# Even shares for the convolutions from slot 36 on, and a step-by-step pace for decoding layer 2's weights

## The chip, the cores and the metric

The kernel runs on one core of one Trainium2 chip. Five engines of that core take part, each with its own queue, in order: TensorE (PE in the profile, with its weight loads as PEld), VectorE (DVE), ScalarE (ACT), GpSimd (POOL) and SyncE (SP), which issues most of the DMAs. [...] The metric is device microseconds of one execution. The kernel before took 1217.21 us, the median of 2 runs (1216.93 to 1217.49).

## The reference

Input x is 2 x 4096 x 192 in float32. Three stages follow one another:

- a causal depthwise convolution of 7 taps: the taps are a softmax of `weight` (8 heads x 7), and each head serves 24 of the 192 channels;
- layer 1, on the 8192 rows: `h = x @ w_in` (192 x 2048), `g = h * clip(h + 3, 0, 6) / 6`, `y = g @ w_out` (2048 x 192);
- layer 2, of the same sizes with its own weights: `h = y @ w_in`, `g = h` where h is positive and `exp(h) - 1` elsewhere, `out = g @ w_out`.

The weights arrive as float64, so a float32 pair of words must be decoded into a float32 on the chip before they can be used.

## The kernel before

**Blocks and slots.** The 8192 rows are cut into 16 blocks of 512 (256 of each batch). In each layer the 2048 hidden columns are cut into 16 tiles f of 128. One slot is one (layer, block, f): `mm1` (L437) makes h of that tile in a PSUM bank, `gate` (L461) turns it into g, `split_g` (L473) splits g into a high part gh and a rest gl, and `mm2` (L482), four slots later (LAG), adds the tile's share of the output. The list `slots` (L497) has 512 entries: slots 0 to 31 hold blocks 0 and 1 of layer 1, interleaved; 32 to 95 hold blocks 2 to 5 of layer 1, 16 slots each; from 96 on layers 2 and 1 alternate by block: layer 2 block 0 in 96 to 111, layer 1 block 6 in 112 to 127, layer 2 block 1 in 128 to 143, and so on.

**Exactness.** Each product is made from high and low parts, so a slot has five matmuls of `mm1` and five of `mm2`. From slot 36 on (BOTH + LAG, L706) they are issued as two streams of half height, lower and upper rows of the array, whose matmuls run side by side; the lower stream is 8 matmuls ahead (BEHIND). There an `mm1` has 5 matmuls in one half and 4 in the other: 19 half matmuls a slot, 9.5 pairs. Three banks hold h (`ps_h`, L100).

**What runs beside the matmuls.** For each slot ACT makes u and gh, DVE g and gl. The rest are jobs, generators whose steps are dealt out slot by slot:

- `weights` (L597): decodes 30 items, 16 of layer 1 and then 14 of layer 2, sorted by the slot in which they are first needed. Items 16, 17 and 18, the first of layer 2, are w_in of tiles 0 to 3, the last 64 rows of w_in of tiles 0 to 7, and w_in of tiles 4 to 7. An item takes four steps: `decode` (L117) scales one word on ACT and shifts the other on DVE (tensor_scalar), then come the rest of the split of the item before, and two DVE combinations. `split_w` (L157) copies the high part on ACT and subtracts on DVE.
- `feed(b)` (L324): 12 DMAs on SP that bring block b of x. `squares(b)` (L270): two DVE transposes. `conv(b)` (L315): 20 steps; `taps_vector` (L275) has one product on ACT and six multiply-adds (acc) on DVE for each of two parts (512 and 256 elements), taken in turn; then come the operands of `mm1`: opA (ACT), opB (DVE), and opC and opD, which need ACT copies (L308 to L312), two DVE subtractions (L313, L314, step 19) and two more ACT copies of their results (L316, L317, step 20).
- the end of a block: `upper_sum` (L362, the rest of the sums y, s and yr) and, for layer 2, `split_y` (L418).

**The planner.** `run_jobs` (L524) is called once a slot, behind g of this slot and gl of the one before. A job has a first slot a, a deadline e and a number of steps n. It is forced in slot e - 2 (e - 1 where e is at most 32). Before slot 112 (OWN) it otherwise gets a step only while the estimated debt of DVE and ACT is low (L535); from slot 112 on it gets its even share of the slots from a to e (L536). Among the jobs that want a step, the one with the earliest deadline goes first. The deadline of `weights` is `when(ready)` (L562), where `ready` is the item last decoded; for layer 2 it rises evenly from slot 40 to 112 (W2). For blocks 2 to 6 the deadline of the convolution is the first slot of its block, but slot 104 for block 6.

The work ahead of slot 36 is not issued in the order of the text: the framework packs it, engine by engine, when the program is built, and there later steps can fill an engine's gaps. From slot 36 on the order is that of the text (`tc.manual_schedule`, L706).

```
        def wanted(jb):
            e, a, _, n, done = jb
            if s >= e() - (1 if e() <= BOTH else 2):
                return True
            if s < OWN:
                return s >= a and debt[0] < 0 and debt[1] < 500
            return done * (e() - a) < n * (s - a + 1)
```

Of the kernel before, what the change touches and what calls it, by code (L numbers as in the profile page):

```python
# [17 lines left out]
P = 128  # L18
LAG = 4
BEHIND = 8  # L20
RA = 6
# [2 lines left out]
FIRST0 = 1  # L24
FIRST = 5
TENSOR_TAPS = 2
OWN = 112
W2 = (40, 112)
R_CUTS = ((4, 4, 8), (8,))
PACE = 1900  # L30
NB = 512
# [26 lines left out]
def conv_moe_moe2(ctx: ExitStack, tc: tile.TileContext, x, weight, w_in1, w_out1, w_in2, w_out2, out):  # L58
# [18 lines left out]
    B, S, D = x.shape  # L77
# [3 lines left out]
    NF = FF // P  # L81
    PAD = K - 1
    G = D // H
    R = D - P
# [29 lines left out]
    def word(raw, i):  # L114
        return raw.rearrange("p (n two) -> p n two", two=2)[:, :, i]

    def decode(raw, n, meanwhile):  # L117

        xw = tmp.tile([P, NB], F32, name="xw", tag="xw")
        act.mul(xw[:, :n], word(raw, 1).bitcast(F32), 2.0 ** -112)
        c = tmp.tile([P, NB], I32, name="cw", tag="cw")
        vec.tensor_scalar(out=c[:, :n], in0=word(raw, 0).bitcast(U32), scalar1=2.0 ** -29, scalar2=7.0,
                          op0=ALU.mult, op1=ALU.min)
        yield
        yield from meanwhile
        xi = xw.bitcast(I32)
        vec.scalar_tensor_tensor(out=c[:, :n], in0=xi[:, :n], scalar=3, in1=c[:, :n],  # L130
                                 op0=ALU.logical_shift_left, op1=ALU.bitwise_or)
        yield
        vec.scalar_tensor_tensor(out=xi[:, :n], in0=xi[:, :n], scalar=SIGN, in1=c[:, :n],
                                 op0=ALU.bitwise_and, op1=ALU.bitwise_or)
        yield
        return xw
# [20 lines left out]
    def split_w(item, f):  # L157

        kind, l, a, e = item
        if kind == "out":
            v = f[:, :(e - a) * D].rearrange("p (f e) -> p f e", f=e - a)
            w = wo[l][:, a:e]
            act.copy(w[:, :, 0:D], v)
            yield
            for c0, c1, to in ((0, P, 2 * P), (P, D, D)):
                vec.tensor_tensor(out=w[:, :, to:to + c1 - c0], in0=v[:, :, c0:c1],
                                  in1=w[:, :, c0:c1].bitcast(F32), op=ALU.subtract)
            yield  # L170
            return
        w = {k: v[:, a * P:e * P] for k, v in wi[l].items()}
        if kind == "in":
            f = f[:, :(e - a) * P]
            act.copy(w["h"], f)
            yield
            vec.tensor_tensor(out=w["l"], in0=f, in1=w["h"].bitcast(F32), op=ALU.subtract)
        else:
            f = f[:, :(e - a) // 2 * P].rearrange("p (f c) -> p f c", c=P)
            r = w["r"].rearrange("p (f two c) -> p two f c", two=2, c=P)  # L180
            for k, h in enumerate((LO, UP)):
                act.copy(r[h, k], f[h])
            yield
            for k, h, o in ((0, LO, UP), (1, UP, LO)):
                vec.tensor_tensor(out=r[o, k], in0=f[h], in1=r[h, k].bitcast(F32), op=ALU.subtract)
        yield
# [83 lines left out]
    def squares(b):  # L270
        for part, t in enumerate(x_sb.pop(b)):
            vec.transpose(out=halves(b, part), in_=t)
            yield
# [31 lines left out]
    def conv_r(b):  # L305
        a = yield from taps_vector(b, 1)
        lh, hl = opnd[0, b][2:]
        T0, T1 = slice(0, HB), slice(HB, NB)  # L308
        act.copy(hl[LO, T0], a[LO])
        act.copy(lh[UP, T1], a[UP])  # L310
        yield
        act.copy(lh[UP, T0], a[LO])  # L312
        act.copy(hl[LO, T1], a[UP])  # L313
        yield  # L314
        vec.tensor_tensor(out=lh[LO, T0], in0=a[LO], in1=hl[LO, T0].bitcast(F32), op=ALU.subtract)  # L315
        vec.tensor_tensor(out=hl[UP, T1], in0=a[UP], in1=lh[UP, T1].bitcast(F32), op=ALU.subtract)  # L316
        yield  # L317
        act.copy(hl[UP, T0], lh[LO, T0].bitcast(F32))
        act.copy(lh[LO, T1], hl[UP, T1].bitcast(F32))
        yield  # L320

    def conv(b):
        opnd[0, b] = ring()
        yield from alternate(conv_main(b, taps_tensor if b < TENSOR_TAPS else taps_vector), conv_r(b))  # L324
# [12 lines left out]
    def feed(b):  # L337
        load_squares(b)
        yield
# [166 lines left out]
    at = {sl: i for i, sl in enumerate(slots)}  # L506
# [11 lines left out]
    def job(gen, n, a, e):  # L518

        jobs.append([e if callable(e) else lambda: e, a, gen, n, 0])  # L520
# [3 lines left out]
    def run_jobs(s, before):  # L524


        for i, (eng, w) in enumerate(zip((vec, act), before)):
            debt[i] = min(max(debt[i] - PACE, -PACE), -PACE // 2) + eng.work - w

        def wanted(jb):  # L530
            e, a, _, n, done = jb
            if s >= e() - (1 if e() <= BOTH else 2):
                return True
            if s < OWN:
                return s >= a and debt[0] < 0 and debt[1] < 500  # L535
            return done * (e() - a) < n * (s - a + 1)  # L536

        while True:
            todo = [j for j in jobs if wanted(j)]
            if not todo:  # L540
                break
            jb = min(todo, key=lambda j: j[0]())
            w = vec.work, act.work
            if next(jb[2], jobs) is jobs:
                jobs.remove(jb)
            jb[4] += 1
            debt[0] += vec.work - w[0]
            debt[1] += act.work - w[1]

    def whole(*gens):  # L550
        for g in gens:
            yield from g
# [5 lines left out]
    def due(item):  # L558
        kind, l, a, e = item
        return at[l, 0, a] + (LAG if kind == "out" else 0)  # L560

    def when(i):  # L562

        if i >= len(items):
            return 0
        if i < N1:
            return due(items[i]) - LEAD
        return min(due(items[i]) - LEAD, W2[0] + (W2[1] - W2[0]) * (i - N1) // (len(items) - N1))

    def cuts(*steps):  # L570
        out, a = [], 0
        for n in steps:
            while a < NF:
                out.append((a, a + n))
                a += n
                if n != steps[-1]:
                    break
        return out

    items = [("in", l, a, e) for l in range(2) for a, e in cuts(*((2, 2, 4) if l == 0 else (4,)))]  # L580
    items += [("r", l, a, e) for l in range(2) for a, e in cuts(*R_CUTS[l])]
    items += [("out", l, a, e) for l in range(2) for a, e in cuts(2)]
    items.sort(key=due)
    N1 = sum(it[1] == 0 for it in items)

    raws = {}
    seen = [0]

    def ahead(i):
        for k in range(i, min(i + 3, len(items))):  # L590
            if k >= seen[0]:
                seen[0] = k + 1
                raws[k] = load_w(items[k])

    ready = [0]

    def prepare():  # L597

        last = iter(())
        for i, item in enumerate(items):  # L600
            ahead(i)
            f = yield from decode(raws.pop(i), (item[3] - item[2]) * {"out": D, "in": P, "r": R}[item[0]], last)
            ready[0] = i
            last = split_w(item, f)
            next(last)
        yield from last
        ready[0] = len(items)

    opnd[0, 0] = ring()
    weights = prepare()  # L610
    d0 = yp.tile([P, NB], F32, name="diag0", tag="y0")
    d1 = yp.tile([P, NB], F32, name="diag1", tag="yr")
    diag = [(d0, d1)[k // 4][:, k % 4 * P:(k % 4 + 1) * P] for k in range(K)]
    main = conv_main(0, taps_tensor)
    with tc.manual_schedule():
# [13 lines left out]
        r = conv_r(0)  # L629
# [7 lines left out]
    drain(transposes(1))  # L637
    drain(main)

    job(weights, 0, 0, lambda: when(ready[0]))  # L640
    job(conv(1), CONV, 0, at[0, 1, 0])
    for b in range(2, NBLK):
        e = at[0, b, 0]
        if b <= RA:
            s = at[0, 1, 2] if b == 2 else at[0, b - 1, 0] if b < RA else at[0, RA - 1, 4]
            t = s + 8
            if b == RA:
                e = at[1, 0, NF // 2]
        else:
            t = at[1, b - RA - 1, NF - 3]  # L650
            e = at[1, b - RA, NF - 3]
        job(feed(b), 1, t - 8, t - 7)
        job(whole(squares(b), conv(b)), 2 + CONV, t, e)
    for b in range(NBLK):
        e = at[1, b, 0]
# [31 lines left out]
    BOTH = at[0, 2, 0]  # L687
# [18 lines left out]
    with tc.manual_schedule():  # L706
        ends = {}
        n = {LO: 0, UP: BEHIND}
# [47 lines left out]
```

## Time and profile before

| | |
|---|---|
| median of 2 runs | 1217.21 us |
| profiled execution | 1217.44 us, of which the span 1215.7 us |
| instructions | 25127 |
| PE busy | 1176.2 us, 97% |
| DVE busy | 945.6 us, 78% |
| ACT busy | 929.9 us, 76% |
| mean granted clock of TensorE | 0.985 |
| HBM | 21 GB/s over the span |

The span runs from the first to the last instruction; 1.7 us of the profiled execution's time lie outside it. Busy time is the union of an engine's instructions. Matmuls overlap, and at half the clock a matmul counts as busy for longer, so a stretch with PE busy is not a stretch at full rate. DVE and ACT instructions overlap a little with the one before them (a DVE instruction of 512 elements lasts 0.68 us, and the next starts 0.60 us after it); where the next start is shown, it is the price.

### The profile page before, as it was taken

To read this page: it belongs to the slowest core of one execution; us is meant where nothing else is said; L and a number is where in the kernel's file an instruction comes from. 1 tells how busy PE (TensorE), PEld (TensorE's weight loads), DVE (VectorE), ACT (ScalarE), POOL (GpSimd) and SP (SyncE) were. 2 spreads that over 40 slices of the span, in tenths; PEclk is the share of its full clock that TensorE was granted. 3 is DMA by queue.
4 is the path that set the end of the run, shared out by engine and by line. 5 is a ranking of instruction groups with operands and counts; after the bars stand their busy time and mean duration, and the time that the engine had idled before them with its cause. 6 is when DMAs were issued, how large, how long until landed. Compare 5 with 4: busy or idle time off the path is not lost.

```text
span 1215.7 us, 25127 instructions
## 1 busy us (share of the span) xinstructions
PE 1176.2 (97%) x9496; PEld 994.9 (82%) x9496; DVE 945.6 (78%) x1607; ACT 929.9 (76%) x1683; POOL 44.6 (4%) x490
## 2 busy tenths in 40 slices
PE   8999889896999999999999999999999999999997
PEld 6788668695898888988798888988889888987776
DVE  8998798886777878777787877778787766776775
ACT  6778567676778696877869687786968778888885
POOL 0000000000000000000000000000000000000000
PEclk9999899898999999999999999999999999999999
DMA  6321111100100101010010100001000000000001
GB/s 164 97 79 31 32 44 48 32 2 1 18 11 1 28 1 28 1 18 11 1 27 2 27 2 16 13 1 27 1 15 2 14 2 2 14 14 14 14 11 18
DMA packets 108091, 26.81 MB, mean 22 GB/s; under 512 B 99648, under 2 KB 106816, under 8 KB 107968
## 3 DMA queue, kind: packets, MB, share of 16 engines
q1 hardware_dynamic: 106320, 24.99, 9.7%
q8 instruction: 74, 1.21, 0.4%
q14 instruction: 49, 0.40, 0.1%
q10 hardware_dynamic: 1648, 0.20, 0.1%
HBM read 18.87 MB, written 6.29 MB: 21 GB/s over the span
## 4 chain that ended last, share of the span: by engine, by line
PE 85%; ACT 7%; DVE 6%; issue 2%; DMA 0%; SPq 0%; ACTq 0%; DVEq 0%
PE p L493 43%; PE h L453 41%; ACT u L52 3%; DVE acc L52 2%; DVE g L52 2%; DVE gl L52 1%; ACT gh L52 1%; ACT y L52 1%; ACT opC L52 1%; ACT opD L52 1%; PE psc L292 1%; DVE s L52 0%; ACT opA L52 0%; ACT yr L52 0%; ACT s L52 0%
## 5 line engine op out<-in xcount | busy, mean ns | idle before, releaser
L493 PE MATMUL p<-gh,wo 64*128 64x512 f32 (+1 forms) x2976 | 658.2, 395 | 0.2 <-ACT gh L52 0.2
L493 PE MATMUL p<-gl,wo 64*128 64x512 f32 (+1 forms) x1984 | 536.3, 395 | 0.0
L52 DVE SCALAR_TENSOR_TENSOR g<-u,h 128x512 f32<-128x512 f32 x512 | 350.5, 685 | 238.1 <-ACT u L52 234.6
L493 PEld LDWEIGHTS p<-gh,wo 64*128 64x128 f32 (+1 forms) x2976 | 466.6, 187 | 52.3 <-ACT gh L52 0.7
L493 PEld LDWEIGHTS p<-gl,wo 64*128 64x128 f32 (+1 forms) x1984 | 362.2, 186 | 34.6 <-DVE gl L52 0.3
L52 DVE TENSOR_TENSOR gl<-g,gh 128x512 fp32r<-128x512 f32 x512 | 350.3, 684 | 0.6 <-ACT gh L52 0.4
L52 ACT CAST gh<-g 128x512 fp32r<-128x512 f32 x512 | 311.5, 608 | 16.7 <-DVE g L52 16.2
L52 ACT ACTIVATE u<-h,three 128x512 f32<-128x512 f32 x256 | 175.8, 687 | 116.4 <-PE h L453 114.1
L453 PE MATMUL h<-opA,wi1h 64*128 64x512 f32 x512 | 200.3, 397 | 9.5 <-DVE g L52 9.2
L453 PE MATMUL h<-opA,wi0h 64*128 64x512 f32 (+1 forms) x476 | 189.8, 403 | 14.1 <-ACT opA L52 14.0
L453 PE MATMUL h<-opA,wi1l 64*128 64x512 f32 x512 | 199.8, 396 | 0.0
L453 PE MATMUL h<-opB,wi1h 64*128 64x512 f32 x512 | 198.4, 393 | 0.0
L52 ACT ACTIVATE u<-h 128x512 f32<-128x512 f32 x256 | 152.4, 595 | 51.6 <-PE h L453 49.3
L453 PE MATMUL h<-opA,wi0l 64*128 64x512 f32 (+1 forms) x476 | 188.8, 400 | 0.0
L453 PE MATMUL h<-opB,wi0h 64*128 64x512 f32 (+1 forms) x476 | 187.9, 398 | 0.2 <-DVE opB L52 0.2
L52 ACT ACTIVATE u<-u 128x512 f32<-128x512 f32 x256 | 161.9, 632 | 8.1
L453 PE MATMUL h<-opD,wi1r 64*128 64x512 f32 x384 | 149.8, 394 | 0.0
L453 PE MATMUL h<-opC,wi1r 64*128 64x512 f32 x384 | 149.8, 394 | 0.0
L453 PE MATMUL h<-opC,wi0r 64*128 64x512 f32 (+1 forms) x366 | 146.1, 401 | 2.1 <-ACT opC L52 2.1
L453 PE MATMUL h<-opD,wi0r 64*128 64x512 f32 (+1 forms) x366 | 144.6, 397 | 0.0
L453 PEld LDWEIGHTS h<-opA,wi1h 64*128 64x128 f32 x512 | 95.1, 186 | 22.4 <-DVE g L52 14.4
L453 PEld LDWEIGHTS h<-opA,wi0h 64*128 64x128 f32 (+1 forms) x476 | 89.0, 187 | 29.7 <-ACT opA L52 15.8
(83 smaller groups left out, 1268.7 us busy)
## 6 DMA issues: line engine op xcount, KB each, us to landing
raw<-in_moe_w_out_dram SPq DMA_DIRECT2D x16, 384.0 KB, 3.2
out_dram<-z SPq DMA_DIRECT2D x186, 32.0 KB, 1.6
raw<-in_moe_w_in_dram SPq DMA_DIRECT2D x7, 512.0 KB, 3.8
x_sq<-in_x_dram SPq DMA_DIRECT2D x112, 32.0 KB, 2.1
raw<-in_moe_w_in_dram SPq DMA_DIRECT2D x8, 256.0 KB, 3.8
xr_sq<-in_x_dram SPq DMA_DIRECT2D x56, 32.0 KB, 2.0
x_sb<-in_x_dram SPq DMA_DIRECT2D x4, 128.0 KB, 3.0
raw<-in_moe_w_in_dram SPq DMA_DIRECT2D x4, 128.0 KB, 3.5
```

The lines of the kernel that those rows point to most:

```text
L52: return fn(*args, **kw)
L292: nc.tensor.matmul(ps[:, n * HB:(n + 1) * HB], diag[k], q[:, n, k:k + HB], start=k == 0, stop=k == K - 1)
L453: mm = nc.tensor.matmul(h, k, m[half], start=low and i == 0, stop=high and i == len(todo) - 1)
L493: nc.tensor.matmul(p, k, m[half], start=first and not end and k is not w0l, stop=last and end == 1)
```

## The change

- The even share (L536) holds from slot 36 (BOTH + LAG) on, no longer from 112; OWN is gone.
- W2 is (30, 112), no longer (40, 112).
- The deadline of `weights` is no longer that of a whole item: `pace` puts the steps of layer 2's items, from the third on, at fifths of the interval between two items' deadlines. `counted` counts the steps.
- For blocks 2 to 6 the convolution's first slot becomes the second slot of the block before (`at[0, b - 1, 1]`: 5, 33, 49, 65, 81), and the deadline of block 6 becomes its own first slot, 112. The feed of a block stays 8 slots ahead of its convolution, and so moves with it.

```diff
-OWN = 112
-W2 = (40, 112)
+W2 = (30, 112)
...
-            if s < OWN:
+            if s < BOTH + LAG:
                 return s >= a and debt[0] < 0 and debt[1] < 500
             return done * (e() - a) < n * (s - a + 1)
...
+    def pace():
+
+        i = ready[0]
+        if i <= N1 or i >= len(items):
+            return when(i)
+        return when(i - 1) + (when(i) - when(i - 1)) * min(steps[0] + 1, 5) // 5
...
     ready = [0]
+    steps = [0]
+
+    def counted(gen):
+        try:
+            while True:
+                next(gen)
+                steps[0] += 1
+                yield
+        except StopIteration as end:
+            return end.value
 
     def prepare():
...
-            f = yield from decode(raws.pop(i), (item[3] - item[2]) * {"out": D, "in": P, "r": R}[item[0]], last)
-            ready[0] = i
+            n = (item[3] - item[2]) * {"out": D, "in": P, "r": R}[item[0]]
+            f = yield from counted(decode(raws.pop(i), n, last))
+            ready[0], steps[0] = i, 0
...
-    job(weights, 0, 0, lambda: when(ready[0]))
+    job(weights, 0, 0, pace)
     job(conv(1), CONV, 0, at[0, 1, 0])
     for b in range(2, NBLK):
         e = at[0, b, 0]
         if b <= RA:
-            s = at[0, 1, 2] if b == 2 else at[0, b - 1, 0] if b < RA else at[0, RA - 1, 4]
-            t = s + 8
-            if b == RA:
-                e = at[1, 0, NF // 2]
+            t = at[0, b - 1, 1]
```

## Rows read from the trace of the kernel before

**Rows 1.** The page: busy time by engine, and the chain that ended last
```profile
PE 1176.2 (97%) x9496; PEld 994.9 (82%) x9496; DVE 945.6 (78%) x1607; ACT 929.9 (76%) x1683; POOL 44.6 (4%) x490
PE 85%; ACT 7%; DVE 6%; issue 2%; DMA 0%; SPq 0%; ACTq 0%; DVEq 0%
```
**Rows 2.** Busy time by stretch: length, PE, PEld, DVE, ACT, POOL, clock, DMA
```profile
108.28:314.08 205.80, 181.12 (x1445) 155.83 (x1444) 166.44 (x297) 140.61 (x264) 7.18 (x76) 0.93 0.12 28
350.41:1195.00 844.59, 844.32 (x7214) 715.84 (x7212) 641.66 (x1043) 677.05 (x1214) 33.40 (x379) 1.00 0.07 11
```
**Rows 3.** The same stretches, tile g alone: two DVE instructions a slot
```profile
108.28:314.08 205.80, 97.62 (x152) 46.38 (x77) 0.93 0.12 28
350.41:1195.00 844.59, 488.60 (x760) 230.51 (x380) 1.00 0.07 11
```
**Rows 4.** Waits of PE, 108.28 to 314.08: total us, times, longest
```profile
PE h L453 <- ACT opA L52: 13.8, 3, 5.3
PE h L453 <- DVE g L52: 9.2, 2, 8.2
PE h L453 <- ACT opC L52: 1.4, 3, 0.5
```
**Rows 5.** Busy time around PE's gaps, columns as in Rows 2
```profile
135.81:142.20 6.39, 5.91 (x24) 3.96 (x26) 2.71 (x5) 3.47 (x8) 0.09 (x1) 0.50 0.00 0
180.89:186.57 5.68, 5.20 (x22) 3.38 (x24) 3.95 (x8) 3.46 (x8) 0.09 (x1) 0.50 0.00 0
219.83:223.79 3.96, 0.01 (x1) 0.00 (x0) 3.67 (x8) 0.67 (x2) 0.00 (x0) 1.00 0.00 0
223.79:230.95 7.16, 6.49 (x28) 4.48 (x30) 4.82 (x10) 4.31 (x10) 0.09 (x1) 0.52 0.00 0
286.92:295.10 8.18, 0.00 (x0) 0.00 (x0) 5.75 (x12) 4.83 (x11) 0.00 (x0) 0.63 0.00 0
295.10:299.22 4.12, 4.12 (x20) 3.27 (x22) 2.98 (x5) 3.10 (x6) 0.09 (x1) 0.50 0.01 4
277.00:281.00 4.00, 2.98 (x27) 2.42 (x25) 1.29 (x2) 3.90 (x8) 0.09 (x1) 1.00 0.00 0
```
**Rows 6.** Timeline of DVE in slot 46, ahead of block 3: start, length, instruction
```profile
130.66 0.68 DVE L52 SCALAR_TENSOR_TENSOR g<-u,h 128x512 f32<-128x512 f32 x1
131.85 3.65 DVE L52 SCALAR_TENSOR_TENSOR acc<-xT,taps,acc 128x256 f32<-128x256 f32 x7
136.40 0.41 DVE L52 TENSOR_TENSOR opC<-acc,opD 64x256 fp32r<-64x256 f32 x1
136.84 0.42 DVE L52 TENSOR_TENSOR opD<-acc,opC 64x256 fp32r<-64x256 f32 x1
```
**Rows 7.** Timeline of ACT in slot 46 (in brackets: idle before, releaser)
```profile
135.15 0.62 ACT L52 CAST opA<-acc 128x512 fp32r<-128x512 f32 x1 [4.18 <-DVE acc L52]
138.22 0.69 ACT L52 ACTIVATE u<-h,three 128x512 f32<-128x512 f32 x1
```
**Rows 8.** Timeline of PE: block 2's first matmul, the last before block 3
```profile
97.89 0.97 PE L453 MATMUL h<-opA,wi0h 128*128 128x512 f32 x3 [0.26 <-ACT opA L52]
130.91 0.39 PE L453 MATMUL h<-opB,wi0h 64*128 64x512 f32 x1
```
**Rows 9.** Timeline of DVE: slot 31, transposes of a block, slot 102
```profile
94.62 1.54 DVE L52 SCALAR_TENSOR_TENSOR acc<-xT,taps,acc 128x256 f32<-128x256 f32 x3
...
269.31 0.70 DVE L52 STREAM_TRANSPOSE xT<-x_sq 128x512 f32<-128x512 f32 x1
...
270.26 0.65 DVE L52 SCALAR_TENSOR_TENSOR g<-u,h 128x512 f32<-128x512 f32 x1
...
284.06 6.43 DVE L52 SCALAR_TENSOR_TENSOR acc<-xT,taps,acc 128x512 f32<-128x512 f32 x12
```
**Rows 10.** Timeline of SP: four DMAs of one feed
```profile
35.78 1.89 SPq L267 DMA_DIRECT2D x_sq<-in_x_dram  x4
```

## The prediction

> **What bounds the kernel now.** First the shares and the chain that ended last: PE is busy 97% and holds 85% of the chain, DVE 6%, and no DMA is on it [rows 1]. So time can only come from stretches in which PE does not run at its full rate. I looked for them with busy time by stretch. From 350 us on PE is never idle and the clock is full [rows 2], and 380 slots (two g instructions each) take 844.59 us: 2.22 us a slot [rows 3]. Slots 36 to 111 are 76 slots and take 205.80 us [rows 3] instead of 76 x 2.22 = 168.9. **36.9 us are lost there**, and that is all that this change can win back, apart from slot 31.
>
> Where they go: PE is idle 205.80 - 181.12 = 24.7 us of the stretch [rows 2]. Its waits name three gaps for opA (13.8 us), 1.4 us for opC right behind them, and 9.2 us for g in two gaps, the larger 8.2 [rows 4]. [...]
>
> The cause is read from slot 46. DVE is in order: behind g at 130.66 come seven taps of block 3's convolution in one go, 3.65 us [rows 6], ACT waits 4.18 us for them before it can make opA [rows 7], and PE, whose last matmul before block 3 started at 130.91 [rows 8], stands. Slots 62 and 78 repeat this for blocks 4 and 5; in slot 102 twelve taps in one go (6.43 us from 284.06 [rows 9]) hold up g, and PE runs out of banks for h at 286.92 [rows 5]. The planner forces the steps there, since the debt let few through before.
>
> **The change, part by part.** *Shares from slot 36 on.* Following the rule, a convolution has 22 steps over 15 slots: after slot s, 22(s - a + 1)/15 of them. That removes the crams: no more than two taps fall in a slot, and opA is made 5 slots ahead of its block. Removed: the 36.9 us. What takes its place:
>
> 1. *DVE is nearly full.* A slot's two gates take 131.85 - 130.66 = 1.19 us [rows 6], 19.1 in 16 slots. A convolution: 6.4 for its taps, 0.95 for its transposes (269.31 to the next g at 270.26) [rows 9], opB 0.6 and opC, opD 0.44 each (start to start [rows 6]): 8.8. The end of a block, three of 512 elements: 1.8. The paced decoding in slots 48 to 63, five instructions per item of 0.2 to 0.6 each, nearly three items: 5.9 (estimate from the 0.6 per 512 elements). Sum 35.6 us, and PE gives 16 x 2.22 = 35.6. So DVE has no room in slots 36 to 79, only from 80 on, where block 6's convolution is spread over 31 slots. Before, 166.44 us of DVE work lay in 205.80 [rows 2]; now some 163, since part of the decoding moves ahead of slot 36, must fit 168.9. Slot by slot (work minus 2.22, never below zero) DVE falls behind where the block's end, two taps and a decoding step meet: slots 53 to 55 ask 3.5, 2.5 and 2.9. How late may it be? In slot 102 the cram began at 284.06 and PE ran until 286.92, 2.9 us on, 1.9 past the 1.0 that a slot has free. The excess over about 2 us falls on PE once each in slots 55 and 73: 0.5 + 0.4 = **0.9 us** (0 to 4, if DVE also waits for ACT at each block's end).
> 2. *The last steps still fall in slot e - 2.* By the share, 20 of 22 steps are done after slot 45; opC and opD's subtractions and the two ACT copies of them come in slot 46, forced. With g starting at T, the gates end at T + 1.2 and the subtractions at T + 2.05; the copies end 138.22 - 137.26 = 0.96 behind the second one [rows 6, 7], so T + 2.6 to 3.0. Block 3 starts on PE at 131.3 - 130.66 = T + 0.64 [rows 6, 8], and its fourth matmul, which needs opC, three pairs of 2.22 / 9.5 = 0.23 later, at T + 1.34. PE waits 1.4 us plus the lateness of DVE, by the sums 0.3, 1.6 and 1.6 in slots 46, 62 and 78: 1.7 + 3.0 + 3.0 = **7.7 us** (4.2 with no lateness, 13 with 2 us more each). At block 6, with DVE at rest, **0.5 us** (0 to 1.7).
> 3. *The block's end in slot 99* gave the smaller gap for g, 9.2 - 8.2 = **1.0 us** [rows 4]; it stays.
>
> *W2 and the pace.* The earlier deadline (30 for item 17) now goes before block 2's convolution (32). Ahead of its taps come item 17's last three steps and item 18's first two: a subtraction 0.6, two combinations 1.2, a shift 0.3, two subtractions 1.2, so 3.3 us of DVE. In slot 31 DVE now has three taps left, 1.54 us [rows 9], and PE waits only 0.26 for opA at 97.89 [rows 8], so the cover is used up. Block 2 starts later by **3.1 us**, between 0 (the packing ahead of slot 36 puts the taps first) and 3.9 (opA and one more copy behind it). Nothing can be gained there beyond the 0.26.
>
> *Feeds.* They move 6 to 11 slots earlier: 12 DMAs at 1.89 / 4 = 0.47 us each on SP [rows 10], 5.7 us in SP's queue. Behind them stand raw loads of weights, issued two items ahead, over 10 slots or 22 us; no engine waits. Cost 0; without that lead, up to 5.7 us once.
>
> *Counting* costs no instruction.
>
> Sum without the clock: 0.9 + 7.7 + 0.5 + 1.0 + 3.1 = 13.2 us.
>
> 4. *The clock.* A gap of 3.96 us was followed by half the clock, one of 1.02 at 279 us was not [rows 4, 5]. The new gaps of 3.1, 1.7, 3.0 and 3.0 us lie between, the three long ones nearer to 3.96. A drop costs 10.9 / 4 = 2.7 us, so 0 to 10.9; I take two drops, **5.4 us**.
>
> [...] In slot 46 ACT stands 4.18 us before opA with u of the next slot queued behind it [rows 7]. [...]
>
> Forecast: the profiled execution of 1217.4 us (span 1215.7 and 1.7 outside, 0.2 above the median) - 36.9 + 13.2 + 5.4 = **1199 us**, or 1199 against the median 1217.2.
>
> **The rivals.**
> - *Clock holds.* The gaps shrink below what lowers the clock: -36.9 + 13.2 gives 1193.7; with the block 2 delay packed away too, 1190.6. For: they are shorter than any gap that was followed by half the clock. Against: three are within 1 us of 3.96.
> - *Full DVE throughout.* Every waiting step adds lateness: bank waits 4 and block starts 13 us, the rest as above (4.6), four drops 10.9: 32.5 of 36.9 are given back, 1213. For: no spare DVE time in 44 slots. Against: from 350 us on DVE is busy 76%, with spread convolutions, and PE is not idle [rows 2].
> - *Slower.* ACT, in order, waits in nearly every slot for a step that DVE made in the same slot; two copies and u then come late, 138.91 - 137.26 = 1.7 us by slot 46 (u starts at 138.22 and lasts 0.69 [rows 7]). It decides from 0.5 us a slot on (36.9 / 76). At 0.7 in each of the 76 slots 53 us take the place of 36.9, with the block 2 delay 1237. [...] Against: the alternation puts most ACT steps one slot behind their input.
> - *Doing nothing* isn't one: from slot 36 on the share rule asks for no debt.
>
> **How the numbers follow.** Forecast 0.50, clock holds 0.28, full DVE 0.17, slower 0.05. What a measurement of this kernel can tell from no change is about 2%, 24 us: faster means below 1193, slower above 1241. Two thirds of the second case (the lower half of its terms) and little of the first lie below 1193: faster 0.22; slower 0.02; within 0.76. The range takes the second case down to 1188 (no drops, block starts without lateness, no block 2 delay is 1187) and the third up to 1213; one in ten is left out on either side.
>
> **What would show it.** Right: no run of seven or twelve taps from slot 36 on; DVE busy above 95% in slots 36 to 79; PE waits for opC (copied by ACT) at the starts of blocks 3, 4 and 5, of 1.5 to 3 us; a wait for opA of about 3 us near 98 us; two of the four followed by half the clock. Wrong: PE idle below 5 us in slots 31 to 111 (no new gaps), or PE short of g banks in most slots (DVE's lateness mis-sized), or a wait at slot 31 unchanged (packing).

## The result, and the profile after

The changed kernel took 1200.62 us (median of 2 runs, 1200.4 to 1200.85) against 1217.21: a ratio of 0.9865, with a 95% interval of 0.9844 to 0.9886. That is 16.6 us less; the forecast was 1199. Measured again beside the other versions, the kernel before took 1216.6 to 1216.7.

The page after, busy time by engine, as in [rows 1]; line numbers are one lower than before:

```profile
PE 1173.4 (98%) x9496; PEld 975.2 (81%) x9496; DVE 943.7 (79%) x1607; ACT 931.4 (78%) x1683; POOL 44.1 (4%) x490
```

The shares hardly move, and would not tell where 16 us went. Busy time by stretch does. The first line below is slots 36 to 79, the second slots 36 to 111 (from g of slot 36 to g of slot 112, the boundaries of [rows 2]):

```profile
111.43:226.05 114.62, 105.58 (x839) 82.41 (x838) 99.49 (x182) 78.95 (x147) 3.90 (x44) 0.96 0.16 37
111.43:297.57 186.14, 176.71 (x1445) 139.53 (x1444) 160.87 (x290) 139.27 (x259) 6.71 (x76) 0.97 0.10 23
```

Slots 36 to 111 take 186.14 us where they took 205.80 [rows 2]. Of the 36.9 us that were lost there, 186.14 - 168.9 = 17.2 are left. PE is idle 9.4 us of it (before 24.7). Against the 19.7 us won stand 3.0 us in slots 26 to 35, which take 29.03 us from g to g and took 26.00. Behind them nothing changed: g of slot 130 to g of slot 508 takes 841.3 us in both.

The waits of PE from 95 us on, as in [rows 4]:

```profile
PE h L452 <- ACT opC L51: 6.8, 4, 2.6
PE h L452 <- ACT opA L51: 1.7, 1, 1.7
PE h L452 <- DVE opB L51: 1.1, 2, 0.8
PE h L452 <- DVE g L51: 1.0, 3, 0.5
```

The gaps of 4 to 8 us are gone. What is left is the wait for the last operands of a block (opC at four block starts, opB), one for opA at block 2 and little for g. PE at the starts of blocks 3 and 4 (the wait for opC at block 3 stands below, in slot 46, and that at block 5 among the stretches that follow):

```profile
136.32 0.50 PE L452 MATMUL h<-opB,wi0h 64*128 64x512 f32 x1 [0.37 <-DVE opB L51]
178.60 0.49 PE L452 MATMUL h<-opB,wi0h 64*128 64x512 f32 x1 [0.77 <-DVE opB L51]
181.01 0.79 PE L452 MATMUL h<-opC,wi0r 64*128 64x512 f32 x1 [1.68 <-ACT opC L51]
```

The granted clock, as in [rows 5] (the third number from the end, a share of the full one): 0.51 behind slot 31 and at the start of block 3 and of block 4, 1.00 in the gap of block 5 and in what follows it:

```profile
101.96:105.37 3.41, 3.41 (x10) 2.67 (x9) 2.60 (x6) 1.67 (x4) 0.00 (x0) 0.51 0.02 6
139.64:142.90 3.26, 3.26 (x16) 2.60 (x18) 1.83 (x4) 1.16 (x2) 0.09 (x1) 0.51 0.45 71
181.01:187.30 6.29, 6.29 (x30) 4.97 (x32) 2.81 (x5) 3.23 (x6) 0.18 (x2) 0.51 0.37 88
220.71:222.86 2.15, 0.00 (x1) 0.00 (x1) 1.63 (x4) 0.83 (x3) 0.00 (x0) 1.00 0.27 42
222.86:228.00 5.14, 5.14 (x44) 4.19 (x46) 2.85 (x5) 3.57 (x7) 0.18 (x2) 1.00 0.00 0
```

Slot 46 after, DVE first, then ACT, then PE, as in [rows 6 to 8] (start, length, instruction; in brackets the idle time before it and its releaser):

```profile
137.08 0.69 DVE L51 SCALAR_TENSOR_TENSOR g<-u,h 128x512 f32<-128x512 f32 x1 [0.82 <-ACT u L51]
...
138.28 0.41 DVE L51 TENSOR_TENSOR opC<-acc,opD 64x256 fp32r<-64x256 f32 x1
138.73 0.42 DVE L51 TENSOR_TENSOR opD<-acc,opC 64x256 fp32r<-64x256 f32 x1
140.33 0.69 DVE L51 SCALAR_TENSOR_TENSOR g<-u,h 128x512 f32<-128x512 f32 x1 [1.18 <-ACT u L51]
```

```profile
134.82 0.67 ACT L51 ACTIVATE xw<-raw 128x512 f32<-128x512 f32 x1
135.51 0.41 ACT L51 CAST opC<-acc 64x256 fp32r<-64x256 f32 x1
135.93 0.40 ACT L51 CAST opD<-acc 64x256 fp32r<-64x256 f32 x1
136.36 0.69 ACT L51 ACTIVATE u<-h,three 128x512 f32<-128x512 f32 x1
...
138.73 0.40 ACT L51 CAST opD<-opC 64x256 fp32r<-64x256 f32 x1 [1.18 <-DVE opC L51]
139.18 0.40 ACT L51 CAST opC<-opD 64x256 fp32r<-64x256 f32 x1
```

```profile
139.64 0.79 PE L452 MATMUL h<-opC,wi0r 64*128 64x512 f32 x1 [2.59 <-ACT opC L51]
```

No taps are left in this slot; its two subtractions (opC, opD) and the two copies behind them are the chain, and PE starts 0.06 us after its end.

### The profile page after: what moved, and what is told of

Read it like the earlier page. It is cut to its first block, busy times and chain, and to the rows that moved or that the text cites. A ratio compares the mean times of both kernels' runs of the same rounds, so it can differ in the third digit from the quotient of the medians.

```text
span 1199.1 us, 25137 instructions
## 1 busy us (share of the span) xinstructions
PE 1173.4 (98%) x9496; PEld 975.2 (81%) x9496; DVE 943.7 (79%) x1607; ACT 931.4 (78%) x1683; POOL 44.1 (4%) x490
## 3 DMA queue, kind: packets, MB, share of 16 engines
HBM read 18.87 MB, written 6.29 MB: 21 GB/s over the span
## 4 chain that ended last, share of the span: by engine, by line
PE 86%; DVE 7%; ACT 5%; issue 1%; DMA 0%; SPq 0%; ACTq 0%; DVEq 0%
PE p L492 44%; PE h L452 41%; ACT u L51 2%; DVE g L51 2%; DVE acc L51 2%; DVE gl L51 2%; ACT gh L51 1%; ACT y L51 1%; PE psc L291 1%; DVE s L51 0%; ACT opC L51 0%; ACT s L51 0%; DMA x_sb<-in_x_dram 0%; DVE cw L51 0%; ACT opD L51 0%
## 5 line engine op out<-in xcount | busy, mean ns | idle before, releaser
L51 DVE SCALAR_TENSOR_TENSOR acc<-xT,taps,acc 128x256 f32<-128x256 f32 (+1 forms) x180 | 106.7, 602 | 0.6 <-ACT acc L51 0.5
```

Of the source, the lines that this page charges most:

```text
L51: return fn(*args, **kw)
```

## The experiments

To compare versions, each row gives what a stretch of slots takes from start of g to start of g, less 2.22 us a slot (844.59 / 380, not rounded; for slots 26 to 35, less the 26.0 of before). The column us is the median; the stretches are those of the traced execution.

| kernel | us | 26-35 | 36-47 | 48-63 | 64-79 | 80-95 | 96-111 |
|---|---|---|---|---|---|---|---|
| before | 1217.2 | 0 | 8.3 | 10.9 | 6.5 | 0.8 | 10.4 |
| after | 1200.6 | 3.0 | 6.2 | 6.2 | 4.4 | 0.5 | -0.1 |
| share alone | 1224.6 | 0 | 10.0 | 12.2 | 13.0 | 5.2 | 3.9 |
| pace and W2 alone | 1217.6 | 1.9 | 8.1 | 10.5 | 10.5 | 1.0 | 5.6 |
| after, whole items | 1210.0 | 1.4 | 8.7 | 12.0 | 3.2 | 2.0 | 2.3 |
| after, W2 from 40 | 1199.5 | 0 | 7.3 | 5.7 | 5.4 | 0.5 | -0.1 |
| after, fewer taps | 1193.0 | 3.0 | 3.0 | 3.6 | 2.4 | 0.5 | -0.1 |
| after, two slots sooner | 1191.4 | 1.9 | 3.3 | 3.0 | 2.4 | 0.4 | -0.5 |
| after, one slot sooner | 1190.6 | 3.0 | 2.8 | 2.9 | 2.3 | -0.1 | -0.5 |
| the same, block 3 from 36 | 1189.9 | 1.9 | 2.7 | 2.9 | 2.3 | -0.1 | -0.5 |
| two slots sooner, W2 from 44 | 1191.2 | 0 | 3.9 | 3.1 | 5.0 | -0.1 | -0.6 |
| one slot sooner, copies on GpSimd | 1207.2 | 1.9 | 7.3 | 8.7 | 8.4 | 0.5 | 0.4 |

### The share rule alone

```diff
-OWN = 112
+OWN = 36
```

(in the kernel before, all else as it was)

> The kernel before (1217.2 us) with one line of the change: the even share from slot 36 on, with the old first slots (8 slots ahead of a block), the old W2 and the decoding in whole items. Theory (a gap at a block's start is the last steps' own 1.4 us plus DVE's lateness): 22 steps in 8 slots ask 2.2 to 5 us of DVE in each of slots 42 to 46, DVE comes about 4 us late to blocks 3, 4 and 5 and their gaps stay at 4 to 5 us with half the clock behind; only block 6, whose cram lay in a stretch with room, gains its 9 to 10 us: 1207 us (1203 to 1211). Rival (the crams were the whole cause, so the share rule alone brings the whole gain): 1200 us.

Measured: 1224.6 us, ratio 1.0061 (1.0044 to 1.0077): slower than before, and against both expectations. The waits of PE in this version:

```profile
PE h L453 <- DVE g L52: 16.5, 10, 3.1
PE h L453 <- DVE opB L52: 5.9, 3, 2.0
PE h L453 <- ACT opA L52: 5.5, 4, 2.1
```

DVE in slot 43, from its gates to the next g:

```profile
125.86 0.68 DVE L52 SCALAR_TENSOR_TENSOR g<-u,h 128x512 f32<-128x512 f32 x1
...
127.18 1.39 DVE L52 TENSOR_TENSOR wi1r<-xw,wi1r 64x512 fp32r<-64x512 f32 x2
128.58 0.69 DVE L52 SCALAR_TENSOR_TENSOR cw<-xw,cw 128x512 int32<-128x512 int32 x1
...
130.18 1.14 DVE L52 SCALAR_TENSOR_TENSOR acc<-xT,taps,acc 128x256 f32<-128x256 f32 x2
131.71 0.69 DVE L52 SCALAR_TENSOR_TENSOR g<-u,h 128x512 f32<-128x512 f32 x1 [0.38 <-ACT u L52]
```

A whole decoding item falls between the taps, g comes 5.85 us after g, and PE waits for it. The theory had the lateness at the block starts (opA, opB) but not the waits for g (16.5 us in all, 10.0 of them ahead of block 5's start), nor that block 6's gain in slots 96 to 111 (10.4 to 3.9) would be spent in slots 80 to 95 (0.8 to 5.2). So sharing over 8 slots is no gain at all. Over 15 slots it is one, even with the decoding in whole items (1210.0 us, below). What the new first slots do without the share was not run.

### Pace and W2 alone

```diff
-            if s < BOTH + LAG:
+            if s < 112:
...
-            t = at[0, b - 1, 1]
+            t = (at[0, 1, 2] if b == 2 else at[0, b - 1, 0] if b < RA else at[0, RA - 1, 4]) + 8
+            if b == RA:
+                e = at[1, 0, NF // 2]
```

> The changed kernel without the share and without the new first slots and deadline of the convolutions: only W2 from 30 and the pace by steps. Theory: seven to nine taps still come in one go ahead of blocks 3, 4 and 5, with gaps of 4 to 6 us; ahead of block 6 four taps in place of twelve, which wins some 8 us; the block 2 delay costs 3: 1213 us (1209 to 1217). Rival (room on DVE from the earlier decoding is what the change won): 1205 us or less.

Measured: 1217.6 us, ratio 1.0011 (1.0001 to 1.0020). The time is that of before, just outside the theory's range; the rival fell. Slots 96 to 111 won 4.8 us (10.4 to 5.6, not 8), and block 5, with nine taps in one go where there had been six, lost 4.0. By itself the share rule makes the kernel 0.6% slower, and the pace with W2 leaves it where it was (0.1%, with an interval that almost reaches zero); with the new first slots they win 1.35% together.

### The decoding in whole items

```diff
-    job(weights, 0, 0, pace)
+    job(weights, 0, 0, lambda: when(ready[0]))
```

> The changed kernel (1200.6 us) with the decoding of layer 2 in whole items again, W2 and the shares as changed. Theory (DVE is full in slots 36 to 79, and its lateness beyond a slot or so falls on PE): the same work comes in lumps of 1.8 to 2.7 us every six slots, slots 51, 57 and 69 ask 4.3 to 5.2 us of DVE, and PE waits for g 1 to 2 us behind each lump: some 4 us more, less 1 us at slot 31, where less decoding goes first: 1203.6 us (1202 to 1206). Rival (only the sum of DVE's work counts): 1200.6 us, within 1.

Measured: 1210.0 us, ratio 0.9949 (0.9934 to 0.9963). The direction is the theory's, the size over twice its 4 us: the pace is worth 9.4 us. The rival (only the sum counts) fell. PE's waits, and slot 51 on DVE:

```profile
PE h L452 <- DVE g L51: 9.8, 10, 2.1
```

```profile
153.48 0.68 DVE L51 SCALAR_TENSOR_TENSOR g<-u,h 128x512 f32<-128x512 f32 x1
...
158.86 0.69 DVE L51 SCALAR_TENSOR_TENSOR g<-u,h 128x512 f32<-128x512 f32 x1 [0.64 <-ACT u L51]
```

g comes 5.4 us after g there. The waits for g grow from 1.0 to 9.8 us in ten places.

### Less work for DVE

```diff
-            vec.scalar_tensor_tensor(out=a, in0=q[:, :, k:k + HB], scalar=taps[:, part, k:k + 1], in1=a,
-                                           op0=ALU.mult, op1=ALU.add)
+            if part or b not in (3, 4, 5) or k % 2:
+                vec.scalar_tensor_tensor(out=a, in0=q[:, :, k:k + HB], scalar=taps[:, part, k:k + 1], in1=a,
+                                         op0=ALU.mult, op1=ALU.add)
```

> The changed kernel without taps 2, 4 and 6 of the 512-element part in blocks 3, 4 and 5 (their values are not the reference's): 2.0 us less DVE work in each of these blocks, every step still in its slot. Theory (a block's start waits 1.4 us for the chain of the last steps, plus DVE's lateness): the waits for opB go, those for opC shrink from 2.6, 1.7 and 2.2 us to 1.4 each at most and do not vanish; waits for g go; one or both half-clock stretches behind them go: 1194.5 us (1192 to 1198). Rival 1 (the lateness is all of it): the waits for opC vanish too, 1189 us. Rival 2 (the chain alone, DVE's work is no matter): the waits stay at 1.7 to 2.6, 1199 to 1200.

Measured: 1193.0 us, ratio 0.9803 (0.9786 to 0.9819).

```profile
PE h L453 <- ACT opC L51: 5.8, 4, 2.0
PE h L453 <- DVE g L51: 0.5, 1, 0.5
PE h L453 <- DVE opB L51: 0.2, 1, 0.2
```

The time is the theory's, and neither rival's. The waits for opB and g nearly go, and the mean granted clock of the traced execution is 0.995, where it was 0.992. But the waits for opC stay at 2.0, 1.7 and 1.7 us, more than the 1.4 that the chain was given, and at block 4 the wait did not shrink at all (1.68 before): in this the second rival was nearer. With DVE relieved, the chain of the last steps costs some 1.8 us a block, and DVE's work the rest.

### The last steps two slots, and one slot, sooner

```diff
-        job(whole(squares(b), conv(b)), 2 + CONV, t, e)
+        job(whole(squares(b), conv(b)), 2 + CONV, t, e - 2 if 3 <= b <= RA else e)
```

(the second with e - 1)

> The changed kernel with the deadline of the convolutions of blocks 3 to 6 two slots earlier, all else the same. Theory (the last two steps fall in slot e - 2, and opC comes too late for the block's fourth matmul): the waits for opC and opB at the starts of blocks 3, 4 and 5 (7.9 us in all) fall below 0.5 each, and the two stretches at half clock behind them (4.8 us lost) go; DVE, still full, gives some 4 us back as waits for g: 1192 us (1189 to 1195). Rival (DVE's whole work is the bound in slots 36 to 79, wherever PE waits): the waits for opC turn into waits for g of the same length: 1197 to 1200 us.

> The changed kernel with the deadline of the convolutions of blocks 3 to 6 one slot earlier (two slots earlier took 1191.4 us). Theory (the chain's own wait is 1.4 us and one slot is 2.2): the last steps then come 0.8 us ahead of need, less the lateness of 0.3 to 1.6: waits for opC of 0 to 0.8 us at the starts of blocks 4 and 5, no half clock; 1192 us (1190.5 to 1194.5), as with two slots. Rival (the wait comes from the DVE work that is packed into the block's end, whatever the slot): about halfway, 1196 us.

Measured: 1191.4 us, ratio 0.9792 (0.9777 to 0.9806), and 1190.6 us, ratio 0.9784 (0.9770 to 0.9799). First PE's waits behind block 2 with two slots, then with one:

```profile
PE h L452 <- DVE g L51: 5.1, 9, 1.4
```

```profile
PE h L452 <- DVE g L51: 2.4, 4, 1.2
PE h L452 <- ACT opC L51: 2.3, 3, 1.3
```

The times are the theory's in both. By the share, an earlier deadline moves every late step of the convolution, not only the last two: with one slot, opA, opB, the two DVE subtractions and the two ACT copies of blocks 3, 4 and 5 all come one slot sooner (opB in slots 44, 60 and 76, the subtractions in 45, 61 and 77). Of the 10.1 us that each traced execution wins (1200.85 to 1190.77 and 1190.73), 8.7 and 9.8 lie behind slot 36; the first has 1.1 more from slots 26 to 35, where its clock was 1.00 behind slot 31's gap (see the last section). The waits for opC and opB go with two slots and shrink with one (1.3 us at block 4, more than the 0.8 expected), and the mean granted clock rises from 0.992 to 0.997 in both; with one slot sooner it is 1.00 from 125 to 150 us, where block 3 starts. One slot is enough. Part of it comes back as waits for g (from 1.0 to 5.1 and 2.4 us), with two slots about the 4 us that the theory named.

### W2 from 40

```diff
-W2 = (30, 112)
+W2 = (40, 112)
```

> The changed kernel (1200.6 us) with W2 back at (40, 112), so that block 2's convolution goes ahead of layer 2's third decoding step again. Theory (slot 31's gap comes from 3.3 us of decoding that went first, and DVE has no room in slots 36 to 79): the 3.0 us that slots 26 to 35 lost come back, PE waits at most 0.5 us for opA near 98 us and there is no half clock there; but the same 3.3 us of DVE work now lie behind slot 36 and lengthen the waits at the starts of blocks 3 to 5 by about as much: 1199 to 1202 us. Rival 1 (the decoding is hidden behind slot 36 too): 1197 us. Rival 2 (the packing ahead of slot 36 decides, not the deadline): the wait near 98 us stays at 1.5 us or more.

Measured: 1199.5 us, ratio 0.9858 (0.9843 to 0.9873).

```profile
PE h L452 <- ACT opA L51: 0.3, 1, 0.3
```

PE's wait at block 2 is all that is shown. The time lies in the theory's range: the wait for opA there falls from 1.7 to 0.3, slots 26 to 35 take 26.0 us again, and of these 3.0 us 1.6 are paid behind slot 36, about half and not nearly all. The 1.1 us between the medians lie within the two intervals: W2 from 30 neither wins nor costs anything that shows.

### Both, with W2 from 44; block 3 from slot 36

```diff
-W2 = (30, 112)
+W2 = (44, 112)
```

(with two slots sooner), and, with one slot sooner and W2 from 30:

```diff
-            t = at[0, b - 1, 1]
+            t = 36 if b == 3 else at[0, b - 1, 1]
```

> Two slots earlier for blocks 3 to 6 (1191.4 us) and W2 = (44, 112) together. Theory: layer 2's decoding no longer goes ahead of block 2's convolution, which gives back the 1.9 us lost in slots 26 to 35; behind slot 36 the decoding fills slots 42 to 48, which the earlier convolution leaves half empty, and DVE's lateness beyond about a slot falls by some 1 us: 1188.5 us (1187 to 1190.5). Rival (the 3.3 us of decoding that come back behind slot 36 are paid there in full): 1191 to 1193 us.

> One slot sooner for blocks 3 to 6 (1190.6 us), and block 3's convolution starts its share in slot 36 in place of 33, so that slot 36 asks 3.3 us of DVE and not 5. Theory (only DVE's lateness beyond a slot falls on PE): the wait for g of 1.2 us near 118 us goes, and since the same steps then crowd into slots 41 to 45 some 0.5 us come back at block 3's start: 1190 us (1189 to 1191.5). Rival (DVE's whole work counts, wherever it lies): no change, with a wait of 1 us or more moved to block 3's start.

Measured: 1191.2 us, ratio 0.9791 (0.9777 to 0.9806), and 1189.9 us, ratio 0.9778 (0.9764 to 0.9791). In the first the rival held: the 1.9 us of slots 26 to 35 are back, and slots 64 to 79 lose 5.0 where they had lost 2.4. In the second the wait for g near 118 us went and 1.2 us for opB and opC stand at block 3's start instead, as its rival said; the time agrees with the theory too, and 0.7 us against one slot sooner is less than the intervals. Behind slot 36 this version and one slot sooner both lose 7.4 us; they differ in slots 26 to 35 (1.9 and 3.0), and one slot sooner had a granted clock of 0.70 over 5.70 us behind slot 31's gap; over the whole span the mean is 0.998 in this version and 0.997 in that. 1189.9 us is the lowest time measured; it beats before and after.

### The last copies on GpSimd

```diff
-        act.copy(hl[UP, T0], lh[LO, T0].bitcast(F32))
-        act.copy(lh[LO, T1], hl[UP, T1].bitcast(F32))
+        copy = nc.gpsimd.tensor_copy if 3 <= b <= RA else act.copy
+        copy(hl[UP, T0], lh[LO, T0].bitcast(F32))
+        copy(lh[LO, T1], hl[UP, T1].bitcast(F32))
```

(with one slot sooner)

> One slot sooner for blocks 3 to 6 (1190.6 us), and for these blocks the last two copies of the chain (opD from opC, opC from opD) run on GpSimd, which is idle but for its relay memsets. Theory (ACT is in order, and u of the next slot stands behind copies that wait for DVE): u and g of the slot behind the last step start about 1 us earlier, the waits for opC of 1.3 and 0.7 us at blocks 4 and 5 shrink below 0.5: 1189 us (1187.5 to 1190.3). Rival (GpSimd's copies come later than ACT's, being slower or behind a relay memset that waits for PE): the waits for opC grow beyond 1.3 us, at 1191 us or more.

Measured: 1207.2 us, ratio 0.9919 (0.9905 to 0.9932): 16.6 us slower than the same kernel with the copies on ACT. Neither expectation had the reason. First PE's waits, then POOL ahead of block 3, then PE behind it:

```profile
PE h L453 <- POOL relay L455: 13.1, 4, 4.7
```

```profile
135.27 0.58 POOL L318 CAST opD<-opC 64x256 fp32r<-64x256 f32 x1 [5.50 <-DVE opC L51]
135.90 0.40 POOL L319 CAST opC<-opD 64x256 fp32r<-64x256 f32 x1
136.24 0.09 POOL L455 MEMSET relay<- 1x1 f32 x1
```

```profile
136.39 0.50 PE L453 MATMUL h<-opA,wi0h 64*128 64x512 f32 x1 [3.56 <-POOL relay L455]
```

GpSimd, 4% busy, carries the memset that tells the upper half of an h bank that the lower half has left it. The copy waits 5.50 us for DVE's opC, the memset of a slot stands behind it, and PE waits for that memset. The copies themselves are no slower than ACT's by much (0.58 and 0.40 us, against 0.40 and 0.40 on ACT in slot 46 of the changed kernel).

## Why the prediction was right, point by point

- **What was to be won** was right: no run of seven or twelve taps is left from slot 36 on, the gaps of 4 to 8 us are gone, and nothing moved outside slots 26 to 111. Of 36.9 us, 19.7 were won there and 3.0 lost ahead of it. Slot 36, which the slot sums did not name, takes 5.0 us from g to g: both transposes and two taps, owed since slot 33, meet a decoding step and a block's end on DVE there. It cost a wait for g of 0.51 us.
- **The last steps in slot e - 2** (7.7 us): the waits for opC and opB at blocks 3, 4 and 5 are 2.97, 2.45 and 2.29 us, together 7.7. Two versions with an earlier deadline for the convolution win 8.7 and 9.8 us behind slot 36, with the clock. That the total came out equal is partly luck, for the split was off: 1.4 for the chain and 0.3, 1.6 and 1.6 for DVE's lateness were forecast, and the largest wait is at block 3, where 1.7 was expected. The chain ends 2.50 us behind g in slot 46 (forecast 2.6 to 3.0), but PE stops at 139.64 - 2.59 = 137.05, level with g, not 1.34 behind it. There g itself is late, because u of slot 46 stood on ACT behind a decoding step and two copies (134.82 to 136.33). That is the slower rival's mechanism, in this slot. In slots 62 and 78 it is DVE that is late: a combination of the decoding and opB stand directly ahead of g (177.39 to 178.46 and 218.76 to 219.83), and PE stops 0.9 us behind g. With DVE relieved 1.8 us a block stay.
- **DVE nearly full** (0.9 us of waits for g): 1.0 measured. The work in slots 36 to 79 is 99.49 us against 97.8 (44 x 2.22) that PE at its rate would give, so the sum that found no room was right. The sign named for it was wrong: DVE is busy 87% there, not over 95%, for the stretch itself grew to 114.62 us, and in 14.1 of the other 15.1 us DVE waits for u.
- **Block 6** (0.5 us): 0.39.
- **Slot 99's gap** (1.0 us, to stay): it went, slots 96 to 111 lose nothing. What failed is the assumption that the end of a block keeps its slots. Before, s and the two copies yr made from it were let through in the same slot, and ACT waited; by the even share yr comes a slot after s. The version with pace and W2 alone, without the share, also has yr a slot after s, and no gap there. ACT before, then after:

```profile
276.82 1.25 ACT L52 COPY yr<-s 64x512 f32<-64x512 f32 x2 [1.45 <-DVE s L52]
```

```profile
271.69 1.25 ACT L51 COPY yr<-s 64x512 f32<-64x512 f32 x2
```

- **Block 2** (3.1 us without the clock): opA's first matmul moved from 97.89 to 100.41, by 2.5 us, but PE's wait rose only from 0.26 to 1.75, where about 3 us were expected, since PE meanwhile ran, up to 98.66, matmuls of `mm2` that before stood behind opA's; the slots cost 1.9 us with two slots sooner, where the clock was 1.00 (below). DVE in slot 31 has ten taps where it had three [rows 9], as the decoding went first:

```profile
94.73 5.38 DVE L51 SCALAR_TENSOR_TENSOR acc<-xT,taps,acc 128x512 f32<-128x512 f32 x10
100.41 0.96 PE L452 MATMUL h<-opA,wi0h 128*128 128x512 f32 x3 [1.75 <-ACT opA L51]
```

- **The clock** (two of four, 5.4 us): three of four. The 2.7 us a drop (10.9 / 4) was the author's estimate, half of the PE busy time that [rows 5] show at a granted clock of 0.50 to 0.52 (5.91 + 5.20 + 6.49 + 4.12 us) over four; no run shows it by itself. In its place the runs showed stretches at 0.51: half of 3.26 and of 6.29 us at blocks 3 and 4, 4.8 together, and 1.1 behind slot 31 (29.03 against 27.93 us for the same slots with two slots sooner, at a clock of 1.00): 5.9.
- **The sum.** 18.6 us were to be given back; the terms measured are 1.0 + 7.7 + 0.4 + 0 + 1.9 + 5.9 = 16.9, and the kernel gave back 36.9 - 16.6 = 20.3. Most of the 3.4 us between lies at the edges of the gaps, for which the sum had no term. The first wait for g shows it:

```profile
116.28 0.39 PE L492 MATMUL p<-gl,wo 64*128 64x512 f32 x1
117.18 0.50 PE L452 MATMUL h<-opA,wi0h 64*128 64x512 f32 x1 [0.51 <-DVE g L51]
117.52 0.40 PE L452 MATMUL h<-opB,wi0h 64*128 64x512 f32 x1
```

The idle time is counted from the end of the last matmul, 0.39 us behind its start, while from 350 us on a pair follows the one before by 0.23 us (2.22 / 9.5); and the first pair behind the gap takes 117.52 - 117.18 = 0.34 us. That is some 0.26 us a gap beyond its idle time, 2.3 us for the nine gaps listed behind slot 36 (an estimate from these rows); the rest may be in stalls too short to be listed. One slot sooner, with a clock of 1.00 from 125 to 150 us, agrees: behind slot 36, 7.4 us are lost, 4.7 of them idle, and its seven gaps give 1.8. So the forecast came within 1.6 us partly by chance: 1.0 for slot 99 and 1.2 of block 2's 3.1 did not come, and these edges did.

- **The rivals.** The clock did not hold, the waits for g came to 1.0 us and those at the block starts to 7.7, not to the 4 and 13 of the full DVE, and ACT's order cost at most a part of these 8.7 us, not 0.7 us in each of 76 slots. The clearest row on order is in the GpSimd version: a memset of 0.09 us stands behind a copy that waits 5.50.

## What to carry to other kernels

Where a cram on one engine makes the gaps, compare the engine's load in each slot, with all that is spread there, with the slot's length before spreading it: the same share over 8 slots with lumps of decoding beside it was slower than the cram (1224.6 us against 1217.2). Then look at the last steps of what was spread: one slot too late, they cost 9.8 us here, over half of what the whole change won. The deadline of a chain that passes through two engines belonged a slot further ahead of its first reader. GpSimd, 4% busy, was not free: with the copies on it PE waited 13.1 us for what stood in its queue.

## What the hardware showed that I had not expected

- The same gap was followed by half the clock in some versions and not in others. In slot 31 PE waits 1.7 us for opA in six versions. In the changed kernel and with one slot sooner the granted clock was then 0.70 over 5.70 us, with two slots sooner 1.00. In slots 26 to 35 fewer taps loses 3.0 us, as the first two do, and block 3 from 36 and the copies on GpSimd 1.9, as the third does; the clock behind their gaps is not shown. Nor is it shown whether it differs between executions of one kernel: the four of two slots sooner took 1190.8 us twice, with a mean clock of 0.997, and 1192.0 us twice, with 0.996, and only one of them, of 1190.8 us, was traced. The 5.70 us behind the gap, after and with two slots sooner (columns as in [rows 2]; the clock is the third number from the end):

```profile
100.41:106.11 5.70, 5.70 (x17) 4.24 (x18) 4.70 (x10) 3.88 (x9) 0.00 (x0) 0.70 0.11 33
```

```profile
100.30:106.00 5.70, 5.65 (x21) 3.82 (x22) 5.58 (x11) 4.77 (x11) 0.00 (x0) 1.00 0.14 31
```

- In the changed kernel, the gap of 2.15 us at block 5 was followed by the full clock (1.00), and that of 1.68 us at block 4, with 0.77 us just ahead of it, by half (0.51) for 6.29 us. A gap's length alone does not say which here; before, each of four gaps of 3.96 us and more was followed by half (0.50 to 0.52) [rows 5].
